# Eight attention batches inside a mixing kernel: scores kept negated and scaled in the keys, e taken a head at a time from PSUM, every sum on VectorE, and a new order

## The chip, the cores and the metric

The kernel runs on one core of one Trainium2 chip. The metric is the device time of one execution in microseconds (us); lower is better. Each time below comes from runs on such a chip, and one further execution was taken with the hardware profiler.

## What is computed

Eight heads of attention over keys and values that are pooled by eight, for eight batches of 576 tokens, and then a mixing block on the 512 channels of the result:

```python
# q, k, v: (8, 8, 576, 64)
k_p = k.reshape(B, H, 72, 8, D).mean(axis=3)
v_p = v.reshape(B, H, 72, 8, D).mean(axis=3)
scores = (1 / sqrt(64)) * q @ k_p.T
scores = scores - scores.max(-1)
attn = exp(scores)
attn = attn / (attn.sum(-1) + 1e-9)
x = (attn @ v_p).transpose(...).reshape(B, S, H * D)
theta = x @ w_theta
zr, zi = x * cos(theta), x * sin(theta)
y = einsum('ts,bsd->btd', w_tok_r, zr) + einsum('ts,bsd->btd', w_tok_i, zi)
u = x + y
out = u + maximum(u @ w_ch, 0)
```

The weights of the mixing block come as 64-bit numbers and are turned into 32-bit ones on the chip, each kept as a high and a low part.

## The kernel before

Each batch is worked in named streams of steps, and a table of words, SCHEDULE, gives the order in which the steps of all streams are issued: `S3.2` is the next step of the softmax of batch 3, tile 2, and a letter behind it (v, g, a) says whether VectorE (DVE), GpSimd (POOL) or ScalarE (ACT) does the step's work where there is a choice. The order on every engine, and much of the choice of engines, is therefore written out in the table; each engine works through its own instructions in that order and waits where an operand or a buffer is not there yet.

The streams: `k`, `v` load keys and values, `K`, `V` pool and place them (`keys` at L581 writes the tile `kpT`), `Q` brings the queries into `qT`, `S` is the softmax (`soften`, L701), `E` turns the weights e (`eraw`, `eh`, `er`) through DMAs, `X` multiplies with the values (`attend`, L904) and copies PSUM to `xT`, `T` forms theta, its sine and cosine and `z` (`rotate`, L958), `Z` splits z into `zh` and `zl`, `M` multiplies with the token weights (`mix`, L1045, matmuls `py`), `F` with w_ch (`final`, L1081, matmuls `pf`) and stores the result by way of a transpose on DVE into `R`. The streams `h`, `w`, `W`, `c` turn the weights at the start.

A softmax tile is 128 tokens (the last of five has 64) by 8 heads by 72 pooled keys. Its scores lie in two PSUM banks, of which there are two such pairs. For batches 2 to 7 a tile goes: largest score per row and head on DVE (`mx`, L762), scores less `mx` on DVE into `e_eps` (L779), one exp over all 576 columns on ACT (L783), sums on DVE (L785), their reciprocals (`ri`, L787), and the division (`en`, L792 on ACT a head at a time, or L796 on DVE or POOL; L803 for the last 8 keys). For batches 0 and 1 ACT takes exp a head at a time from PSUM, with the negated and scaled `mx` as bias, and gives the sums by its accumulator (L767 to L775). `e_eps` is one buffer, held from the first write of e to the last read of the division, and its 73rd column holds 1e-9, so that a sum over 73 columns has the small constant in it.

Four single PSUM banks serve all other matmuls. `xT` has two buffers: the copy of `pv` of batch b + 2 into `xT` (L932 on ACT, L934 on DVE) waits until the last transpose into `R` of batch b has read it (L1128).

Of the kernel before, what the change touches and what calls it, by code (L numbers as in the profile page):

```python
# [35 lines left out]
S0.1 w1.0a S0.1v S0.3 S0.4 w1.0a w0.1g h2 w1.1a w1.0a W0 h2v V0v V0 h2 w1.1a S0.4 Q1.1 S0.2 S0.2a w1.0 X0.0.0 X0.0.1
w1.1 K1.1g h3v S0.2 S0.2v w2.0v v1.0 S0.4 w2.0v X0.0.2 w1.0 h3 Q1.0 S0.3v w1.1 X0.0.1a S0.3g X0.0.2a X0.0.0a X0.0.3 K1
W0a w1.0v X0.0.3a h3v w1.1v K1a w2.1 S0.4 W1 T0.0g h3 w4.0 S0.4g w2.0a k1.2 W0 W1a S0.4g S0.3 S0.3v Q1.1 W1 S0.3 Q1.1a
Q1.0 T0.1a T0.0g T0.1v W0 S0.3a W0v S0.4 V1.0g w3.0a T0.0 Q1.0a S0.4v Q1.2 w2.1a W1 w2.0 w3.0a w2.1a w2.1v v1.1 S0.4
w2.1 w2.1 T0.0 w3.1a w2.1v T0.1 w3.0v S0.4a w2.0 w3.1v w3.1a X0.2.2 X0.2.3 T0.0 T0.0 T0.1 w2.0g T0.0 X0.2.2a X0.2.1  # L40
w3.1 K1.2g T0.1 Q1.3 V1.1g W1a T0.0a w3.1 w3.0 T0.0 X0.2.3a W0 X0.2.0 T0.0 T0.1 T0.1 X0.2.1v w3.0 T0.1a T0.0 X0.2.0a
T0.2a W1 T0.3a Q1.2 T0.1 W2 Q1.3 w3.1v Q1.2v w4.0v T0.3v V1a c0 T0.2v w4.0a w4.0a T0.1 w4.0 w3.0v Q1.3a T0.2 w4.0 W2a
Q1.4 X0.2.3g T0.2 T0.1 T0.3 T0.2 W2 c0a c0a T0.2 c0 T0.4g T0.4g T0.2 T0.3 T0.2a w4.0g W3 T0.2 T0.4 W3a T0.3 c0 T0.2
T0.3 c0 T0.3 T0.2 T0.3a K1 W2 W3 T0.4 T0.4 K1a T0.4 Q1.4 c1 T0.4 c0g W2v T0.3 c0g c0g W2 W4 V1g T0.4 T0.3 c1a T0.4
T0.3 c1a S1.0 Z0.1a Z0.0g W4v S1.0 k2.2 W4 c1 M0.1.0 Z0.1v c1 K2.2v W4a M0.1.0 M0.0.0 c1 W4 S1.0 W4a S1.0 M0.1.0
# [1216 lines left out]
```

## Time and profile before

| | |
|---|---|
| time, median of 3 runs | 567.87 us (567.5 to 568.3) |
| the profiled execution's own time | 568.15 us |
| its span | 566.3 us |
| busy PE / DVE / ACT / POOL | 546.2 / 455.6 / 330.6 / 373.2 us |
| DMA, mean over the span | 102 GB/s |

PE is TensorE's matmuls, PEld its weight loads, SP the engine that issues most DMAs. The profiled execution took 0.28 us more than the median. A row of the profile names the source line (L1058), the engine, the operation, the tile written and those read, sizes, a count and times; in brackets stands how long the engine was idle before the instruction, and what released it.

### The profile page before, as it was taken

What the parts mean: (1) busy time and instruction counts of PE and PEld (TensorE: products, weight loads), DVE (VectorE), ACT (ScalarE), POOL (GpSimd) and SP (SyncE); (2) the same over time, 40 slices, a digit from 0 to 9 for tenths busy, and PEclk for the clock granted to TensorE, in tenths of its full rate; (3) what the DMA queues carried; (4) which work ended last, traced back from release to release, by engine and by line L of the source; (5) the groups of instructions that cost most, each with busy time, mean ns of one, the idle gap of its engine ahead of it and who ended that gap; (6) DMA issues with size and microseconds to landing.
All of it is one profiled execution on the core that took longest, in us unless ns stands there. A gap on an engine that the chain in (4) does not pass through costs nothing.

```text
span 566.3 us, 11646 instructions
## 1 busy us (share of the span) xinstructions
PE 546.2 (96%) x4084; PEld 515.1 (91%) x4084; DVE 455.6 (80%) x867; ACT 330.6 (58%) x774; POOL 373.2 (66%) x526
## 2 busy tenths in 40 slices
PE   5999989999999999999989999999999999999996
PEld 5867779989999998999989999999999999999996
DVE  6999999899888798888868897987879888366164
ACT  3889988887766885566424767446354644334010
POOL 3766665587887987799867596649357766652430
PEclk9999999999999999999989999999999999999999
DMA  9988121556486775358645374543626251200017
GB/s 264 264 288 192 48 72 71 127 114 120 80 153 97 154 115 112 71 122 147 117 91 105 61 127 93 107 85 67 94 43 108 49 82 26 48 1 14 10 22 125
DMA packets 231801, 57.84 MB, mean 102 GB/s; under 512 B 218688, under 2 KB 220352, under 8 KB 231744
## 3 DMA queue, kind: packets, MB, share of 16 engines
q1 hardware_dynamic: 226768, 56.47, 49.4%
q10 hardware_dynamic: 4976, 0.64, 0.7%
q8 instruction: 32, 0.52, 0.4%
q14 instruction: 25, 0.20, 0.1%
HBM read 37.81 MB, written 9.44 MB: 83 GB/s over the span
## 4 chain that ended last, share of the span: by engine, by line
PE 66%; DVE 10%; DMA 8%; SPq 6%; POOL 4%; issue 3%; ACT 1%; DVEq 0%; POOLq 0%; ACTq 0%
PE py L1058 32%; PE pt L970 12%; PE pf L1091 11%; PE pv L923 4%; PE s L728 3%; PE px L984 2%; DMA kpst<-in_k_dram 2%; SPq L878 2%; DMA WTh_st<-in_moe_w_theta_dram 2%; DMA wraw<-in_moe_w_tok_r_dram 2%; DMA vpst<-in_v_dram 1%; SPq L608 1%; DMA out_dram<-R 1%; SPq L629 1%; DVE en L803 1%
## 5 line engine op out<-in xcount | busy, mean ns | idle before, releaser
L1058 PE MATMUL py<-WTh,zh 128*128 128x288 f32 x576 | 81.8, 288 | 1.7 <-ACT zh L206 1.7
L1058 PE MATMUL py<-WTh,zl 128*128 128x288 f32 x576 | 83.0, 292 | 0.0
L1058 PE MATMUL py<-WTl,zh 128*128 128x288 f32 x576 | 81.2, 287 | 0.0
L191 POOL TENSOR_TENSOR zl<-z,zh 128x256 fp32r<-128x256 f32 (+2 forms) x80 | 63.5, 825 | 22.3 <-ACT zh L206 13.2
L1058 PEld LDWEIGHTS py<-WTh,zh 128*128 128x128 f32 x576 | 74.8, 189 | 2.4 <-ACT zh L206 1.9
L1058 PEld LDWEIGHTS py<-WTh,zl 128*128 128x128 f32 x576 | 76.2, 193 | 0.1
L1058 PEld LDWEIGHTS py<-WTl,zh 128*128 128x128 f32 x576 | 74.8, 189 | 0.2
L976 ACT ACTIVATE g<-pt,c_magic 128x512 f32<-128x512 f32 x35 | 24.0, 687 | 52.9 <-PE pt L970 40.9
L1068 DVE TENSOR_TENSOR xT<-py,xT 128x288 f32<-128x288 f32 x64 | 27.9, 444 | 28.4 <-PE py L1058 28.0
L191 POOL TENSOR_TENSOR ul<-xT,uh 128x288 fp32r<-128x288 f32 x42 | 34.0, 823 | 22.1 <-DVE uh L208 12.2
L1091 PE MATMUL pf<-uh,chh 128*128 128x288 f32 x256 | 43.7, 293 | 0.0
L1091 PE MATMUL pf<-uh,chl 128*128 128x288 f32 x256 | 41.9, 286 | 0.0
L1091 PE MATMUL pf<-ul,chh 128*128 128x288 f32 x256 | 41.8, 286 | 0.0
L970 PE MATMUL pt<-th,xh 128*128 128x512 f32 x148 | 39.4, 389 | 0.6 <-POOL Vl L191 0.6
L1098 DVE SCALAR_TENSOR_TENSOR xT<-pf,xT 128x288 f32<-128x288 f32 x64 | 28.1, 446 | 14.5 <-PE pf L1091 14.1
L728 PE MATMUL s<-kpT,qT 128*128 128x144 f32 x256 | 36.9, 288 | 1.9 <-ACT kpT L206 0.8
L970 PE MATMUL pt<-th,xl 128*128 128x512 f32 x148 | 38.2, 381 | 0.2 <-DVE xl L964 0.2
L792 ACT ACTIVATE en<-e_eps,ri 128x64 f32<-128x64 f32 (+1 forms) x120 | 30.3, 335 | 13.3 <-DVE ri L787 9.5
L970 PE MATMUL pt<-tl,xh 128*128 128x512 f32 x148 | 38.0, 379 | 0.0
L762 DVE TENSOR_REDUCE mx<-s 128x8 f32<-128x576 f32 (+2 forms) x42 | 29.9, 715 | 9.6 <-PE s L728 9.4
L1091 PEld LDWEIGHTS pf<-uh,chh 128*128 128x128 f32 x256 | 36.1, 190 | 0.6
L728 PEld LDWEIGHTS s<-kpT,qT 128*128 128x128 f32 x256 | 33.6, 190 | 3.1 <-issue 1.1
(268 smaller groups left out, 1438.8 us busy)
## 6 DMA issues: line engine op xcount, KB each, us to landing
out_dram<-R SPq DMA_DIRECT2D x112, 72.0 KB, 2.1
kpst<-in_k_dram SPq DMA_DIRECT2D x15, 512.0 KB, 4.1
vpst<-in_v_dram SPq DMA_DIRECT2D x28, 256.0 KB, 3.8
qsst<-in_q_dram SPq DMA_DIRECT2D x96, 72.0 KB, 2.4
eraw<-G SPq DMA_DIRECT2D x96, 60.0 KB, 2.2
eraw<-G SPq DMA_DIRECT2D x96, 40.0 KB, 2.0
WTh_st<-in_moe_w_theta_dram SPq DMA_DIRECT2D x4, 512.0 KB, 7.1
wcraw<-in_moe_w_ch_dram SPq DMA_DIRECT2D x4, 512.0 KB, 3.4
```

Source lines behind the costliest of these rows:

```text
L191: nc.gpsimd.tensor_tensor(out[:, r], a[:, r], b[:, r], op)
L728: nc.tensor.matmul(scs[c // 2][:n, 2 * SP * (c % 2) : 2 * SP * (c % 2 + 1)], qT[:, c, t0 : t0 + n], kpT[:, c, :], start=True, stop=True,)
L762: nc.vector.tensor_reduce(mxv, scv, AX.X, ALU.max)
L792: nc.scalar.activation(en[:n, GM * h : GM * h + GM], e[:n, h, 0:GM], AF.Copy, scale=ri[:n, h : h + 1])
L878: nc.sync.dma_start(blocks(Ex, jj, i), blocks(Gx, i, jj))
L923: nc.tensor.matmul(as_written(pv[:, :gn]) if pair else pv[:, :gn], l, by_turns(r) if pair else r, start=i == 0, stop=i == len(terms) - 1,)
L970: nc.tensor.matmul(as_written(pt), l[:, c, :], by_turns(r[:, c, :]), start=i == 0, stop=i == 11)
L976: nc.scalar.activation(halves(g), in_order(pt), AF.Identity, bias=c_magic)
L1058: nc.tensor.matmul(as_written(py[:, :n]), l[:, kk, :], by_turns(r[:, kk, t]), start=i == 0, stop=i == 3 * NK - 1,)
L1068: nc.vector.tensor_tensor(halves(u), in_order(py[:, :n]), halves(u), ALU.add)
L1091: nc.tensor.matmul(as_written(pv[:, :n]), l[:, kk, o], by_turns(uhl[r][:, kk, t]), start=i == 0, stop=i == 11,)
L1098: nc.vector.scalar_tensor_tensor(halves(oT), in_order(pv[:, :n]), 0.0, halves(oT), ALU.max, ALU.add)
```

## The change

Keys are multiplied by -1/64 when they are copied from PSUM into `kpT` (new helper `scaled`; on DVE or ACT). The scores then come out negated and scaled, so the row's minimum takes the maximum's place, exp is taken of minus the score plus that minimum, and neither the subtraction nor the negation of `mx` is needed. For every batch e is taken a head at a time from PSUM on ACT (eight instructions a tile), without the accumulator; all sums are DVE reductions. With `EACH` always true, the branch with the subtraction is never taken. The table is another one throughout: the order of all steps and the engines of many.

```diff
-EARLY, EXACT, V_ON_PE, K_ON_PE, Q_ON_PE, SUMS_ON_ACT = 2, 1, 1, 1, 2, 2
+EARLY, EXACT, V_ON_PE, K_ON_PE, Q_ON_PE, SUMS_ON_ACT = 2, 1, 1, 1, 2, 0
+EACH = lambda b, m: True
...
+    def scaled(e, out, src, by):
+        if e == "a":
+            nc.scalar.activation(out, src, AF.Copy, scale=by)
+        else:
+            nc.vector.tensor_scalar(out, src, by, None, ALU.mult)
...
     def keys(b):
+        by = -1.0 / (POOL * math.sqrt(D))
...
-        copy(e, kpT[0:64, :, 0:SP], heads[:, 0::2])
-        copy(e, kpT[64:128, 0:3, SP:], heads[:, 1::2])
+        scaled(e, kpT[0:64, :, 0:SP], heads[:, 0::2], by)
+        scaled(e, kpT[64:128, 0:3, SP:], heads[:, 1::2], by)
...
         for scv, mxv, _, _ in views:
-            nc.vector.tensor_reduce(mxv, scv, AX.X, ALU.max)
+            nc.vector.tensor_reduce(mxv, scv, AX.X, ALU.min)
...
-        if b < SUMS_ON_ACT:
-            nc.scalar.mul(mx[:n], mx[:n], -scale)
+        if each:
             yield
+            sums = dict(accum_out=sm[:n]) if b < SUMS_ON_ACT else {}
             for x in range(8):
                 j, y = at(x)
                 nc.scalar.activation(
                     e[:n, x], scs[j][:n, SP * y : SP * y + SP], AF.Exp,
-                    bias=mx[:n, x : x + 1], scale=scale, accum_out=sm[:n, x : x + 1],
+                    bias=mx[:n, x : x + 1], scale=-1.0, **{w: s[:, x : x + 1] for w, s in sums.items()},
                 )
-            nc.scalar.activation(sm[:n], sm[:n], AF.Identity, bias=c_eps[:n])
...
+        if b >= SUMS_ON_ACT:
+            if split:
+                nc.vector.tensor_reduce(sm[:n], e[:n], AX.X, ALU.add)
+                nc.vector.tensor_scalar(sm[:n], sm[:n], 1e-9, None, ALU.add)
+            else:
+                nc.vector.tensor_reduce(sm[:n], e_eps[:n], AX.X, ALU.add)
```

Three places where the order moves follow. The first is DVE where batch 4's first copies into `xT` wait for batch 2's last transposes into `R`: `en_4` is the last softmax tile of batch 4, `mx_2` and `sm_2` belong to batch 5. Before:

```order
L785 TENSOR_REDUCE sm_4_3771<-e_eps 64x8
L787 RECIPROCAL ri_4_3917<-sm_4_3771 64x8
L796 TENSOR_TENSOR en_4_3919<-e_eps,ri_4_3917 64x512
L1128 STREAM_TRANSPOSE R_3_3887<-xT_2220 128x288
L1128 STREAM_TRANSPOSE R_2_3922<-xT_2220 128x288
L803 TENSOR_TENSOR en_4_3919<-e_eps,ri_4_3917 64x64
L1128 STREAM_TRANSPOSE R_2_3922<-xT_2220 128x288
L812 STREAM_TRANSPOSE G<-en_4_3919 64x4x128
L815 STREAM_TRANSPOSE G<-en_4_3919 64x64
L762 TENSOR_REDUCE mx_2_3941<-s_2_3882 128x8
L779 TENSOR_TENSOR e_eps<-s_2_3882,mx_2_3941 128x8x72
L785 TENSOR_REDUCE sm_2_3943<-e_eps 128x8
```

and the change, in the same place:

```order
L801 TENSOR_REDUCE sm_4_3715<-e_eps 64x8
L803 RECIPROCAL ri_4_3974<-sm_4_3715 64x8
L1114 SCALAR_TENSOR_TENSOR xT_2290<-pf_3_0_3950,xT_2290 128x288
L1144 STREAM_TRANSPOSE R_3_3980<-xT_2290 128x288 x2
L771 TENSOR_REDUCE mx_2_3984<-s_2_3967 128x8
L950 TENSOR_SCALAR xT_3924<-pv_0_2_3925 128x256
L828 STREAM_TRANSPOSE G<-en_4_4011 64x4x128
L831 STREAM_TRANSPOSE G<-en_4_4011 64x64
L771 TENSOR_REDUCE mx_3_4072<-s_3_3900 128x8
L801 TENSOR_REDUCE sm_2_3986<-e_eps 128x8
```

The division of `en_4` has left DVE (POOL does both parts of it now), the subtraction L779 is gone, the next tile's minimum comes ahead of this tile's sum, and one of the four copies into `xT` has come to DVE.

The second is ACT at the same place, with `xT<-pv` the copies of batch 4. Before:

```order
L783 ACTIVATE e_eps<-e_eps 64x8x72
L206 CAST zh_2_3926<-z_3531 128x1152
L932 ACTIVATE xT_3891<-pv_0_0_3929 128x256
L932 ACTIVATE xT_3891<-pv_0_1_3892 128x256
L783 ACTIVATE e_eps<-e_eps 128x8x72
L932 ACTIVATE xT_3891<-pv_0_3_3974 128x256
L206 CAST uh_4002<-xT_2946 128x288
```

and the change:

```order
L948 ACTIVATE xT_3924<-pv_0_1_3930 128x256
L948 ACTIVATE xT_3924<-pv_0_0_3945 128x256
L209 CAST zh_0_4039<-z_3577 128x1152
L781 ACTIVATE e_eps<-s_2_3967,mx_2_3984 128x72 x8
L209 CAST uh_4139<-xT_3013 128x288
L781 ACTIVATE e_eps<-s_3_3900,mx_3_4072 128x72 x8
L948 ACTIVATE xT_3924<-pv_0_3_4024 128x256
```

Where one exp of 576 columns stood, eight of 72 stand, and the second block of eight stands ahead of the copy of `pv_0_3`.

The third is SP at the start of the program, where the loads of the first keys (`kpst`, `early`, `kprst`), of the first weights (`WTh_st`, `wraw`) and of the first queries (`qsst`) are issued. Before:

```order
L519 DMA kpst_0_117<-in_k_dram 128x2x512
L519 DMA early<-in_k_dram 128x2x512
L387 DMA WTh_st<-in_moe_w_theta_dram 128x1024
L438 DMA wraw_0_144<-in_moe_w_tok_r_dram 128x1152
L531 DMA kprst_149<-in_k_dram 64x512
L629 DMA qsst_0_163<-in_q_dram 128x8x64
```

and the change:

```order
L447 DMA wraw_0_117<-in_moe_w_tok_r_dram 128x1152
L528 DMA kpst_0_119<-in_k_dram 128x2x512
L396 DMA WTh_st<-in_moe_w_theta_dram 128x1024
L540 DMA kprst_128<-in_k_dram 64x512
L528 DMA early<-in_k_dram 128x2x512
L396 DMA WTh_st<-in_moe_w_theta_dram 128x1024
```

The token weights have gone from fourth place to first, and the second load of keys from second to fifth.

## Rows read from the trace of the kernel before

**Rows 1.** The page, parts 1 and 2: busy time by engine, busy tenths in 40 slices.

```profile
PE 546.2 (96%) x4084; PEld 515.1 (91%) x4084; DVE 455.6 (80%) x867; ACT 330.6 (58%) x774; POOL 373.2 (66%) x526
...
DVE  6999999899888798888868897987879888366164
...
PEclk9999999999999999999989999999999999999999
```

**Rows 2.** Busy time (instructions) of PE, PEld, DVE, ACT, POOL in seven stretches.

```profile
0.00:30.00 30.00, 22.71 (x182) 19.95 (x183) 23.70 (x50) 18.29 (x79) 16.14 (x26) 1.00 1.01 262
30.00:80.00 50.00, 47.16 (x284) 36.25 (x283) 48.78 (x84) 46.08 (x100) 33.90 (x43) 1.00 0.55 156
80.00:150.00 70.00, 68.55 (x531) 65.16 (x530) 63.73 (x129) 56.44 (x174) 47.22 (x74) 1.00 0.48 102
150.00:280.00 130.00, 128.26 (x969) 122.45 (x967) 109.62 (x203) 86.89 (x193) 109.77 (x154) 1.00 0.66 122
280.00:300.00 20.00, 18.08 (x144) 17.64 (x143) 15.42 (x25) 5.22 (x9) 13.21 (x20) 0.91 0.39 76
300.00:560.00 260.00, 259.53 (x1972) 252.22 (x1971) 192.10 (x375) 117.70 (x222) 152.97 (x212) 1.00 0.38 65
560.00:566.00 6.00, 1.90 (x15) 1.43 (x13) 2.22 (x8) 0.00 (x0) 0.00 (x0) 0.93 0.59 122
```

**Rows 3.** Timeline 278 to 296: start, us, instruction, idle before it and releaser.

```profile
281.96 3.09 POOL L191 TENSOR_TENSOR zl<-z,zh 128x384 fp32r<-128x384 f32 x4
281.97 4.53 DVE L803 TENSOR_TENSOR en<-e_eps,ri 64x64 f32<-64x64 f32 x1
...
285.02 2.20 POOL L191 TENSOR_TENSOR vpst<-vpst 128x256 f32<-128x256 f32 x3
...
286.98 0.66 ACT L932 ACTIVATE xT<-pv 128x256 f32<-128x256 f32 x2 [9.00 <-DVE R L1128]
...
287.42 0.38 PE L923 MATMUL pv<-eh,Vh 128*128 128x256 f32 x1 [1.92 <-ACT xT L932]
...
288.42 4.05 PE L1058 MATMUL py<-WTh,zl 128*128 128x288 f32 x18
```

**Rows 4.** Chain that ended last, 370 to 490: start, us, what.

```profile
375.72 2.21 PE py L1058 x18
```

**Rows 5.** Groups by line, softmax on DVE: count, busy us, mean ns, idle before.

```profile
L762 DVE TENSOR_REDUCE mx<-s 128x8 f32<-128x576 f32 x30 | 22.4, 746 | 9.6 <-PE s L728 9.4
...
L779 DVE TENSOR_TENSOR e_eps<-s,mx 128x576 f32<-128x576 f32 x24 | 18.2, 758 | 1.7 <-ACT en L792 0.3
L785 DVE TENSOR_REDUCE sm<-e_eps 128x8 f32<-128x584 f32 x24 | 18.0, 750 | 3.7 <-ACT e_eps L783 3.7
```

**Rows 6.** The same groups on ACT.

```profile
L792 ACT ACTIVATE en<-e_eps,ri 128x64 f32<-128x64 f32 (+1 forms) x120 | 30.3, 335 | 13.3 <-DVE ri L787 9.5 <-DVE G L815 3.6
...
L783 ACT ACTIVATE e_eps<-e_eps 128x576 f32<-128x576 f32 (+1 forms) x30 | 20.5, 685 | 20.8 <-DVE e_eps L779 20.6
L771 ACT ACTIVATE e_eps<-s,mx 128x72 f32<-128x72 f32 (+1 forms) x64 | 19.4, 331 | 0.0
...
L767 ACT ACTIVATE mx<-mx 128x8 f32<-128x8 f32 (+1 forms) x10 | 2.0, 200 | 4.4 <-DVE mx L762 4.4
```

**Rows 7.** Timeline of the start, PE and ACT.

```profile
5.01 3.75 PE L575 MATMUL kpp<-kpst,ident 128*128 128x128 f32 x16 [5.01 <-DMA kpst<-in_k_dram]
...
78.83 1.37 PE L1058 MATMUL py<-WTh,zh 128*128 128x288 f32 x9 [1.73 <-ACT zh L206]
...
9.50 0.78 ACT L356 ACTIVATE wsrc_a<-wraw 128x576 f32<-128x576 f32 x1 [4.35 <-DMA wraw<-in_moe_w_tok_r_dram]
```

**Rows 8.** Per line: count, ns of one as min/median/max, of three DVE lines.

```profile
L779 DVE TENSOR_TENSOR e_eps<-s,mx x30: 749/758/760, 126.5 to 476.1; 128x576 f32<-128x576 f32 x24, 64x576 f32<-64x576 f32 x6
L803 DVE TENSOR_TENSOR en<-e_eps,ri x19: 175/482/4531, 87.4 to 471.3; 128x64 f32<-128x64 f32 x15, 64x64 f32<-64x64 f32 x4
L1075 DVE TENSOR_TENSOR ul<-xT,uh x22: 431/454/1290, 127.2 to 550.0; 128x288 fp32r<-128x288 f32 x22
```

More of the change, by code (lines that the diff above doesn't have):

```diff
@@ L36 @@
[L36 to L45, printed above, removed]
@@ new lines @@
+S1.1 S1.1 Q2.0 M0.2.1 S1.1a S1.4 Z0.3g S1.1 X1.0.0 S1.2a V2.2g S1.2v M0.2.1 X1.0.2 k2.0 M0.2.0 M0.2.1 K2.0g Q2.0
+X1.0.1 X1.0.2v X1.0.0v X1.0.1v S1.3 S1.3 S1.2 S1.4 X1.0.3 X1.0.3a S1.2a S1.2 M0.3.1 M0.0.1a T1.0g S1.2 S1.3a k2.1
+M0.3.1 S1.3v T1.0g Q2.0 S1.4 M0.3.1 S1.3 S1.3v M0.3.1 S1.3 T1.0 M0.2.1a S1.4 K2.1v M0.3.0 S1.3 S1.2a T1.0 M0.3.1a
+T1.1g M0.0.0a Q2.1 T1.0 M0.3.0 S1.3a S1.2 S1.4g v2.0 S1.4g K2 S1.3 T1.1g M0.3.0 T1.0 K2v S1.4 T1.0 T1.0a M0.3.1g
+M0.3.0 M0.1.1v M0.3.0g M0.0.0g T1.0 V2.0g S1.4v Q2.1 S1.4 S1.4 S1.4a v2.1 T1.0 T1.0 M0.1.0g S1.4 T1.1 X1.2.1 k3.2 K2
@@ new lines @@
+T2.2a V3 E3.2 F1.0.1 T2.1 F1.0.0 F1.1.0 T2.1a S3.0g T2.1 F1.1.1 F1.0.0 E3.2 F1.3.1 T2.3g T2.1 T2.2g T2.2 F1.1.1 S3.1
+E3.2 T2.1 Q4.0 T2.3g F1.1.1 S3.1 F1.0.1 V3g F1.3.1 F1.2.0 T2.2 T2.2 V3g E3.2g S3.1 F1.3.0 E3.2a F1.3.0 T2.2 F1.1.1
+Q4.1 K4 T2.2 T2.2a F1.2.0 S3.0 E3.2g F1.2.1 T2.2 T2.2 E3.2g F1.2.1 T2.2 F1.3.0 S3.1g T2.3 K4a F1.2.1 Q4.1 F1.2.0
+F1.3.1 T2.3 v4.0 S3.1v X3.2.2 X3.2.2a X3.2.3 T2.3 X3.2.0 X3.2.0v X3.2.3a X2.2.3g X3.2.1 S3.1 X3.2.1a X3.2.3a E3.0 T2.3
+T2.3 T2.4v T2.3a Q4.1 T2.3 T2.3 K4.2g T2.4g K4 T2.4 T2.3 Z2.0v Z2.0v E3.0 K4a v4.2 T2.4 S4.1 T2.4 S4.0 S4.1 T2.4
@@ new lines @@
+v5.0 T3.0 S4.2a K5 M2.3.0 K5a M2.1.0v T3.1g Q5.0 M2.3.0a S4.3 T3.2v E4.0 S4.2g E4.0 T3.0 T3.0 M2.2.1 M2.2.1 M2.2.0
+T3.0a K5 E4.0 V4v T3.0 M2.2.1g M2.2.0 S4.3 T3.0 V5.0g T3.1 K5v M2.2.0v M2.1.0v M2.0.0v T3.0 T3.2g T3.3v T3.1 T3.1
+M2.3.0g T3.1 T3.1 T3.1a T3.1 M2.3.1 V4 M2.3.1 T3.2 M2.2.0g M2.3.1 E4.0 S4.4 F2.1.0 T3.1 T3.1 M2.0.1g M2.3.1 T3.2
+F2.0.0 F2.1.0 S4.2 T3.2 T3.3g V4g T3.4a M2.2.1g T3.2 M2.3.1a F2.0.0 M2.3.1v T3.2 Q5.1 F1.3.1 E4.0v S4.3 F2.1.0 T3.2a
+T3.2 E4.0a Q5.1 V4g F2.1.1 F2.0.1 E4.0g E4.0g T3.2 F2.0.1 F2.0.1 v5.2 F2.1.1 T3.3 T3.2 F2.1.1 v5.1 F2.3.1 T3.3 T3.3
@@ new lines @@
+T4.1 F3.0.1 F3.3.0 F3.3.1 F3.3.0 F3.0.0 S5.1 V5v T4.2g Q6.1 T4.1 F3.0.1 V6.0g F3.2.0 T4.2 T4.1 F3.3.1 T4.1v T4.1 K6
+T4.1 F3.1.1 E5.2a S5.1 T4.1 S5.0 F3.1.0 F3.1.1 F3.2.1 F3.2.0 T4.2 K6a T4.2 T4.2 E5.2g E5.2g T4.3g T4.2 E5.2g F3.2.1
+F3.2.1 T4.3 V5g T4.2a T4.2 v6.1 T4.2 T4.2 K6 F3.2.0 S5.1g X5.2.3 F3.3.1 F3.3.0 K6v T4.3 X5.2.3a X5.2.2 X5.2.1 T4.3
+Q6.1 S5.1v X5.2.0 X5.2.2a X5.2.0v T4.3 T4.3 S6.1 S5.1 X5.2.1a T4.3a X5.2.3g T4.4v T4.3 S6.0 T4.4g T4.3 T4.4 T4.3 T4.4
+E5.0 Z4.0v T4.4 T4.4 Z4.0g Z4.0g T4.4 Z4.0g T4.4a T4.4 T4.4 V6.1g M4.0.0 E5.0 T4.4 E5.0 Z4.0v M4.0.0 M4.0.1 M4.0.0
@@ new lines @@
+S6.2 T5.1 S6.3 M4.3.0g T5.3v E6.0 S6.4 S6.2g M4.0.0g T5.1 Q7.0 T5.2 M4.3.1 T5.1a M4.3.1 S6.2v M4.2.0g E6.0 E6.0g
+M4.0.0g T5.1 T5.1 S6.3 M4.1.1g M4.0.1v M4.2.1 E6.0g V6g T5.1 T5.2 T5.4a Q7.1 T5.2 M4.3.0v T5.2 M4.2.1 F4.3.0 k7.1
+F3.3.1 Q7.1 T5.2 M4.3.1 K7.1g S6.3 T5.2v M4.3.1g v7.0 M4.2.1 T5.2 k7.2 T5.3 V6 F4.1.0 T5.2 M4.2.1g M4.2.1g T5.2 S6.2
+F4.3.0 F4.1.0 M4.3.1v T5.3 T5.3 F4.0.0 F4.0.0 E6.0g F4.1.0 T5.3 T5.3 K7 T5.3a F4.3.1 K7a F4.1.1 T5.3 F4.3.0 F4.0.1
+T5.3 T5.3 V6g F4.3.1 S6.3g F4.1.1 F4.1.1 Z5.0g F4.2.1 S6.3g K7.2g M5.0.0 Q7.1 S6.4 K7 Z5.0g F4.3.1 F4.1.1 K7v S6.3
@@ new lines @@
+S7.4 F4.2.1 F4.2.0 V6v F4.2.0 S7.2 S6.4 F4.0.1 S6.4v E6.0g F4.2.0 F4.3.1 M5.0.0 Z5.1a M5.0.0 S6.4g M5.0.1 F4.0.0
+M5.0.1 F4.0.1 X6.0.0 M5.0.1 M5.0.0 S7.2 Z5.1g X6.0.1 F4.2.1 S7.2 M5.0.1 Z5.3g X6.0.0v X6.0.2 X6.0.3 S6.4 M5.1.0
+X6.0.1a S7.3 M5.1.0 v7.2 X6.0.3v M5.3.0 F4.0.1 E6.2 X6.0.2v E6.2 S7.3 S7.2 M5.1.0 Z5.3g E6.2 M5.3.1 S7.2a S7.2v T6.1g
+M5.1.1 M5.1.0 M5.0.1v S7.3 T6.0v T6.1v M5.1.1 S7.0 S7.3 M5.1.1 Z5.2a M5.0.0v S7.4 V7.2v Z5.2v M5.3.0 T6.0g M5.1.1 T6.0
+T6.0 V7.0g E6.2 S7.2 S7.3v M5.3.1 E6.2v T6.0 M5.3.1 M5.3.1 S7.3g E6.2g M5.2.0 M5.3.0 M5.2.1 M5.2.0 M5.2.0 M5.2.1 S7.4
@@ new lines @@
+F6.2.1 F6.2.0 T7.1 Z7.0v F6.0.0 Z7.2g M7.2.0 M7.0.0 F6.1.0 M7.2.0 Z7.2v M7.2.0 M7.2.0 M7.0.0 F6.1.1 M7.2.1 Z7.0v
+F6.2.0 M7.0.0 F6.3.0 M7.2.1 M7.2.1 Z7.1g M7.0.1 M7.2.1 M7.0.1 F6.3.1 F6.1.0 M7.2.1v F6.3.0 Z7.1v F6.3.0 M7.1.0 F6.3.1
+M7.0.1 M7.2.0a M7.1.0 M7.1.1 M7.0.0 M7.1.1 M7.1.0 Z7.3v M7.3.0 M7.0.0v Z7.3v M7.1.0 M7.1.0v F6.0.0 M7.3.1 M7.2.0g
+M7.3.0 M7.3.0 M7.3.1 M7.1.1 M7.0.0v M7.3.0 M7.3.0g M7.1.1 F6.0.1 M7.0.1 M7.3.1 M7.0.1a M7.1.0g M7.3.0v M7.3.1 F6.0.1
+M7.3.1v F7.1.0 F7.0.0 M7.3.1v M7.1.1a F7.0.0 M7.1.1g F6.1.1 M7.0.1v F7.1.0 F6.2.1 M7.2.1v F6.2.0 F6.2.1 F7.1.0 F7.1.0
@@ L590, in keys @@
         heads = pk[0:64].rearrange("p c x -> p (c x)")[:, 0 : 7 * SP].rearrange("p (h g) -> p h g", g=SP)
-        copy(e, kpT[0:64, :, 0:SP], heads[:, 0::2])
-        copy(e, kpT[64:128, 0:3, SP:], heads[:, 1::2])
-        copy(e, kpT[64:128, 3, SP : 2 * SP - GM], pk[0:64, 3, P - GR :])
+        scaled(e, kpT[0:64, :, 0:SP], heads[:, 0::2], by)
+        scaled(e, kpT[64:128, 0:3, SP:], heads[:, 1::2], by)
+        scaled(e, kpT[64:128, 3, SP : 2 * SP - GM], pk[0:64, 3, P - GR :], by)
         yield
@@ L597, in keys @@
         yield
-        copy(pick(), kpT[64:128, 3, 2 * SP - GM :], pr[0:64, 0:64])
+        scaled(pick(), kpT[64:128, 3, 2 * SP - GM :], pr[0:64, 0:64], by)
         yield
@@ L706, in soften @@
         nt, mi = len(tiles), m - tiles[0]
-        scale = 1.0 / (POOL * math.sqrt(D))
         split = b == 0 and m % 2
@@ L761, in soften @@
         for scv, mxv, _, _ in views:
-            nc.vector.tensor_reduce(mxv, scv, AX.X, ALU.max)
-        if b == 0:
+            nc.vector.tensor_reduce(mxv, scv, AX.X, ALU.min)
+        each = b < SUMS_ON_ACT or EACH(b, m)
+        if not each and b == 0:
             yield
         sm = work([P, 8], F32, "sm", f"sm{b}_{m}", bufs=2)
-        if b < SUMS_ON_ACT:
-            nc.scalar.mul(mx[:n], mx[:n], -scale)
+        if each:
             yield
+            sums = dict(accum_out=sm[:n]) if b < SUMS_ON_ACT else {}
             for x in range(8):
@@ L772, in soften @@
                     e[:n, x], scs[j][:n, SP * y : SP * y + SP], AF.Exp,
-                    bias=mx[:n, x : x + 1], scale=scale, accum_out=sm[:n, x : x + 1],
+                    bias=mx[:n, x : x + 1], scale=-1.0, **{w: s[:, x : x + 1] for w, s in sums.items()},
                 )
-            nc.scalar.activation(sm[:n], sm[:n], AF.Identity, bias=c_eps[:n])
+            if sums:
+                nc.scalar.activation(sm[:n], sm[:n], AF.Identity, bias=c_eps[:n])
             yield
@@ L782, in soften @@
             yield
-            nc.scalar.activation(e[:n], e[:n], AF.Exp, scale=scale)
+            nc.scalar.activation(e[:n], e[:n], AF.Exp, scale=-1.0)
             yield
-            nc.vector.tensor_reduce(sm[:n], e_eps[:n], AX.X, ALU.add)
+        if b >= SUMS_ON_ACT:
[4 more added lines that the diff above has]
+                nc.vector.tensor_reduce(sm[:n], e_eps[:n], AX.X, ALU.add)
         ri = work([P, 8], F32, "ri", f"ri{b}_{m}", bufs=2)
```

167 lines of the change are left out of this document (71 added, 96 removed).

## The prediction

> **What bounds the kernel now.** I began with the page's parts 1 and 2 [rows 1]. PE is busy 546.2 us of a span of 566.3, DVE 455.6, POOL 373.2, ACT 330.6. The change does not touch the list of matmuls (the same products, in another order), so all that it can win or lose lies in the some 20 us in which PE is idle, and in stretches where PE's clock is low. A busy share alone tells nothing of those 20 us, so I next cut the span into seven windows [rows 2]. PE idles 7.3 us in 0 to 30, 2.8 in 30 to 80, 1.45 in 80 to 150, 1.7 in 150 to 280, 1.9 in 280 to 300, 0.5 in 300 to 560 and 4.1 in the last 6. Three things are to be seen. From 300 on, PE is busy 259.53 of 260 us at full clock: nothing can be won there, only lost. From 30 to 80, DVE is busy 48.78 of 50 us and ACT 46.08: there these two set the pace, until the first `py` starts at 78.83 us, after a wait of 1.73 us on ACT's `zh` [rows 7]. And only one window has a low mean clock, 280 to 300 with 0.91.
>
> The timeline of that window [rows 3] shows why. DVE's `en` of 64x64 (L803) starts at 281.97 and takes 4.53 us; POOL runs `zl` and then `vpst` from 281.96 on. Behind that division on DVE stands a transpose into `R`, the last reader of the `xT` buffer; ACT waits 9.00 us for it before the copy of `pv` at 286.98, and PE waits 1.92 us for ACT. [...]
>
> **The change part by part.** The profiled execution took 568.15 us, 0.28 more than the median of the runs; the sum is made against 568.15.
>
> *The stall at 282 to 292.* In the new order `en_4` is on POOL, whole, and the two transposes that stood around it on DVE are no longer split by it. Then PE's wait (1.92) and the slow `py` (4.05 − 2.21 = 1.84) go: **−3.8 us**. Late next there is ACT: its copy of `pv_0_3` now stands behind a second block of eight exps, some 2 us (below). Only one of four copies waits for that block, and PE has `py` and `pf` to work on meanwhile, so I take nothing off. Bounds: 0 if another late hand-over takes its place, −3.8 if none does.
>
> *The scaled keys.* The copies to `kpT` are the same in number, with a multiplication in place of a plain copy. No row shows the price of that, but these are PSUM reads of one pass like the plain copies, which have no second operand tile either: 0, and at worst one L767 (200 ns, ACT's multiplication of a small tile [rows 6]) for each of a batch's four, under 1 us a batch and beside PE.
>
> *The softmax of batches 2 to 7.* DVE loses 30 subtractions of 0.758 us (24 of the large shape make 18.2 us, the six small ones cost as much by their minimum of 749 [rows 5, 8]): 30 × 0.758 = −22.7. It gains the sums of batches 0 and 1, ten at 0.750 [rows 5], +7.5. ACT pays eight exps of 72 columns for one of 576. The plain one takes 0.685 [rows 6]. The nearest rows to the new ones are L771, 19.4 us busy for 64, 0.303 each with the accumulator, and L792, 30.3 for 120, 0.253 each, 64 columns without it. The new ones have no accumulator, so I take 0.253: 8 × 0.253 = 2.0 us a tile, +1.3 for each of 30 tiles, +40 us on ACT; the other end is 8 × 0.303 = 2.4. In batches 0 and 1 ACT loses the accumulator, its ten small multiplications L767 (2.0 us [rows 6]) and ten additions. The chain of a tile goes from minimum, subtraction, exp, sum (0.746 + 0.758 + 0.685 + 0.750 = 2.94) to minimum, eight exps, sum (0.746 + 2.0 + 0.750 = 3.5), 0.56 us longer. From 150 us on the cover is PE's own queue: between the scores of one tile and those of the next PE has `py`, `pf` and transposes to do, of which 18 `py` alone are 2.21 us [rows 4], and there are two pairs of score banks. From 300 to 560 DVE has 68 us idle and ACT 142 [rows 2]. So I cost this at **0** there. Were the cover gone, 30 × 0.56 = 17 us would be the price. `e_eps` stays one buffer: where DVE's subtraction waited for the last tile's division, ACT's exps now do, and behind them on ACT stand `xT` copies and `zh`, for which PE waits. That is a rival below.
>
> *The start.* Ahead of the first `py` DVE has five sums more (+3.7 at 0.750 [rows 5]), and against them copies into `qT`, `eraw` and `Ve`, three scalings of `th` and two of `wsrc_a` that now go to ACT or come later. Summed over all instructions that differ, each at the mean of its like in the trace, DVE's work ahead of the first `py` falls by 0.6 us and ACT's rises by 0.1. POOL's falls. DVE is the fullest there (48.78 of 50 [rows 2]), so: **−0.6 us**. The DMA queue gives both bounds. `wraw` first, ahead of `kpst`, ends ACT's wait of 4.35 us for it at 9.50 [rows 7], of which ACT, nearly as full as DVE, might make 2 us of gain. But PE's first work waits 5.01 us for `kpst` [rows 7], and `wraw`'s 128 × 1152 words of four bytes, 576 KB, now go ahead of it: at the 262 GB/s of the first 30 us [rows 2] that is up to 2.2 us later. Between −2 and +2.2 the count of DVE's work is the nearest.
>
> *80 to 280.* PE idles 3.2 us here in all [rows 2], which is the most that a better order could give back: −3. Ahead of a same count of matmuls DVE has some 6 us less to do (part of the subtractions, filled only partly with work from POOL) and ACT some 3 us more; ACT has 13.6 us free of 70 in 80 to 150 [rows 2]. I take **0**, with −3 and +4 (one stall as in rows 3) as bounds.
>
> *300 to the end.* PE is full; the last 4.1 us (the store of the last result) stay. **0**.
>
> The sum: 568.15 − 3.8 − 0.6 = 563.8, against the median 563.5. I forecast **563.6 us**; with the bounds of start and middle its own range is 560.5 to 566.
>
> [...] The rows show L803, which reads `e_eps` and `ri` from SBUF, once at 4531 ns where its median is 482 [rows 8], while POOL reads SBUF; L1075, also of two SBUF tiles, once at 1290 with a median of 454; and L779, whose one operand is in PSUM, never above 760 in 30 [rows 8]. [...]
>
> **The rivals.** *The same time, by new stalls* (0.16). An order drawn anew can put a late hand-over where there was none: one more like that of rows 3 gives back 3.8 us, so 567 to 569. For it: 30 of the tiles' chains are 0.56 us longer, and PE has no slack to make up for what it loses. Against it: six batches in sequence follow one pattern, and the old order had a single such place.
>
> *Slower, by blocked divisions and additions on DVE* (0.16). By the new order DVE has 179 two-operand instructions with both operands in SBUF, before 140: 39 more, and 30 fewer with one in PSUM. In the trace of before, those of the first kind are the ones with outliers (4531 and 1290 [rows 8]), those of the second have none. The mechanism: a blocked instruction on DVE ahead of the last `R` transpose of a batch, with the `xT` copy, and so PE, waiting behind. It decides once the block outlasts what PE has queued: in rows 3 a delay of 4.5 us cost 3.8. If two of the five such hand-overs (batches 3 to 7, with that of batch 4 gone) are hit, 563.8 + 2 × 3.8 = 571.4 us. Against it: 39 more in 140 is a quarter, and one such hit was seen in all of before, so two are few times as likely as none.
>
> *Slower, by ACT* (0.14). In 80 to 150 ACT is busy 56.44 of 70 us [rows 2]; the new exps add 1.3 us a tile in front of copies of `pv` and of `zh`, and they wait in order for `e_eps`. If four such copies come 2 us late (one block of exps each) with PE waiting, 563.8 + 8 = 571.8. It decides where a block stands directly ahead of a copy that PE needs within 2 us, as with `pv_0_3`. For it: PE's first `py` waits on ACT already [rows 7]. Against it: from 150 on ACT idles a third and more [rows 2]. [...]
>
> **How the numbers follow.** My forecast has 0.54. About 0.2% (1.1 us) is what a measurement here can tell from no change. Faster by more is below 566.7: the forecast's own range, 0.54. Within 0.2%: the first rival, 0.16. Slower: the two rivals by DVE's blocks and by ACT (0.16 and 0.14), 0.30. The range reaches down to 559.5 (all bounds of gain together: 568.15 − 3.8 − 2 − 3 = 559.4) and up to 571.5, which takes in the blocked DVE and leaves out ACT's worse half.
>
> **What would show it.** Right: no DVE instruction of over 2 us around the copies of batch 4, PE's clock at 1.00 all through 150 to 560, `e_eps<-s,mx` near 0.25 us each, the first `py` at about 78, PE idle under 1 us from 300 to 560. Wrong: a window of 20 us after 150 with a mean clock below 0.95 or over 1 us of PE idle, released by ACT's `xT` copy (then look whether a DVE instruction of two SBUF operands or a block of exps stands ahead of it); or a first `py` after 80 us, with `kpst` as the releaser of PE's first work.

## The result, and the profile after

The change is slower: 573.29 us median of 4 runs (572.08 to 575.91) against 567.8 before, a ratio of 1.0098 with a 95% interval of 1.007 to 1.0126. The profiled execution took 573.11 us with a span of 571.3, 5.0 more than before.

The page's part 1 and the clock row of part 2, for the change:

```profile
PE 548.5 (96%) x4084; PEld 518.4 (91%) x4084; DVE 460.1 (81%) x883; ACT 348.0 (61%) x877; POOL 342.2 (60%) x488
...
PEclk9999989999999999999999999899989999999999
```

Its stretches, in the columns of [rows 2]:

```profile
30.00:80.00 50.00, 47.04 (x292) 36.53 (x291) 47.68 (x86) 47.86 (x108) 29.76 (x37) 0.99 0.53 149
80.00:150.00 70.00, 69.30 (x529) 66.33 (x528) 62.69 (x128) 61.92 (x176) 53.81 (x82) 0.98 0.49 102
150.00:280.00 130.00, 127.52 (x968) 122.57 (x967) 112.08 (x212) 91.18 (x240) 94.64 (x137) 1.00 0.65 119
280.00:300.00 20.00, 20.00 (x166) 19.46 (x165) 14.83 (x30) 8.17 (x26) 11.98 (x16) 1.00 0.48 91
300.00:560.00 260.00, 255.18 (x1911) 247.41 (x1910) 196.04 (x371) 119.94 (x283) 139.72 (x199) 0.99 0.36 63
```

Up to 280 us nothing is lost: PE's 196.82 us between 80 and 280, for 1497 matmuls, stand against 196.81, for 1500, in [rows 2]. The old stall is gone, 280 to 300 is full at clock 1.00. The loss is after 300, where PE had been full: it is now busy 255.18 of 260 us. It lies in two places, which the clock row shows as its 8s in the slices that begin at 357 and 414 us (the 8 in the slice from 71 us lies around the first `py`, ahead of the loss). The same view, cut around them:

```profile
352.00:366.00 14.00, 12.18 (x87) 11.99 (x86) 11.64 (x24) 11.10 (x34) 5.37 (x8) 0.88 0.62 124
404.00:422.00 18.00, 15.57 (x122) 14.90 (x121) 14.75 (x23) 2.42 (x10) 13.19 (x17) 0.91 0.33 55
```

The timeline of the second place (columns as in [rows 3]):

```profile
410.56 0.29 POOL L194 TENSOR_TENSOR en<-e_eps,ri 64x64 f32<-64x64 f32 x1 [1.95 <-DVE ri L803]
410.67 3.79 DVE L812 TENSOR_TENSOR en<-e_eps,ri 64x512 f32<-64x512 f32 x1
410.82 3.09 POOL L194 TENSOR_TENSOR zl<-z,zh 128x384 fp32r<-128x384 f32 x4
...
413.90 1.56 POOL L211 CAST zh<-z 128x1152 fp32r<-128x1152 f32 x1
414.38 1.18 DVE L1144 STREAM_TRANSPOSE R<-xT 128x288 f32<-128x288 f32 x3
415.50 0.41 DVE L1084 TENSOR_TENSOR xT<-py,xT 128x288 f32<-128x288 f32 x1
...
415.96 0.38 PE L939 MATMUL pv<-eh,Vh 128*128 128x256 f32 x1 [1.75 <-DVE xT L1084]
...
417.35 0.58 PE L939 MATMUL pv<-eh,Vh 128*128 128x256 f32 x1 [0.68 <-DVE xT L1084]
```

The division of batch 6, tile 4 (the row of 64x512) takes 3.79 us on DVE; the six others of its line in the change take 0.69 to 1.29, and the same division undisturbed takes 0.73 (below, label pool_behind). It ends at 414.46, 0.55 us after POOL's four `zl`, a little less than its free length. Behind it on DVE stand three transposes and the addition of `py` into `xT`, which frees the PSUM bank that the next `pv` needs. PE waits 1.75 and 0.68 us, and from 416 to 422 us the granted clock reads 0.72, where it read 1.00 from 404 to 416.

The first place, one batch earlier:

```profile
358.75 0.73 DVE L510 TENSOR_TENSOR vprst<-vprst 64x256 f32<-64x256 f32 x2 [0.50 <-DMA vprst<-in_v_dram]
...
359.30 3.11 POOL L194 TENSOR_TENSOR zl<-z,zh 128x384 fp32r<-128x384 f32 x4 [0.49 <-ACT zh L209]
...
359.51 0.90 DVE L515 TENSOR_TENSOR vpr<-vprst 64x64 f32<-64x64 f32 x1
360.34 0.76 DVE L819 TENSOR_TENSOR en<-e_eps,ri 128x64 f32<-128x64 f32 x1
361.03 0.44 DVE L1084 TENSOR_TENSOR xT<-py,xT 128x288 f32<-128x288 f32 x1
...
361.52 0.38 PE L939 MATMUL pv<-eh,Vh 128*128 128x256 f32 x1 [1.82 <-DVE xT L1084]
```

Two small DVE instructions beside POOL's `zl` take 0.90 and 0.76 us here, and PE waits 1.82 us for the addition behind them; the clock reads 0.63 from 361.4 to 366, after 1.00 from 352 to 361.4.

Against the same matmuls in the run with both places mended (below, label both), the change needs 44.43 us in place of 40.67 from the start of the 177th `pv` to that of the 1081st `py`, and 40.80 in place of 36.53 from there to the 209th `pv`: 3.8 and 4.3 us. The start of the change:

```profile
6.66 3.76 PE L584 MATMUL kpp<-kpst,ident 128*128 128x128 f32 x16 [6.66 <-DMA kpst<-in_k_dram]
...
78.14 1.47 PE L1074 MATMUL py<-WTh,zh 128*128 128x288 f32 x9 [1.97 <-POOL zh L211]
```

PE's first matmul is 1.65 us later than in [rows 7], the first `py` 0.7 earlier. From the start of the last matmul to the end of the span it is 4.7 us where it was 3.5. In all: −0.7 (start) −3.8 (282 to 292) +3.8 +4.3 (the two places) +1.2 (end) = +4.8, of the 5.0 seen between the two profiled executions.

### The profile page after: what moved, and what is told of

The parts are those of the page before. It is cut to its first block, busy times and chain, and to the rows that moved or that the text cites. A ratio compares the mean times of both kernels' runs of the same rounds, so it can differ in the third digit from the quotient of the medians.

```text
span 571.3 us, 11725 instructions
## 1 busy us (share of the span) xinstructions
PE 548.5 (96%) x4084; PEld 518.4 (91%) x4084; DVE 460.1 (81%) x883; ACT 348.0 (61%) x877; POOL 342.2 (60%) x488
## 4 chain that ended last, share of the span: by engine, by line
PE 68%; DVE 9%; SPq 6%; ACT 6%; POOL 4%; DMA 3%; issue 3%; DVEq 0%; ACTq 0%; POOLq 0%
PE py L1074 30%; PE pf L1107 12%; PE pt L986 10%; SPq L894 5%; PE s L737 5%; PE pv L939 4%; PE px L1000 2%; PE kpp L584 1%; DMA kpst<-in_k_dram 1%; DMA vprst<-in_v_dram 1%; PE s L729 1%; ACT wsrc_a L365 1%; PE vpp L584 1%; SPq L1159 1%; DVE sm L801 1%
## 5 line engine op out<-in xcount | busy, mean ns | idle before, releaser
L1074 PE MATMUL py<-WTh,zh 128*128 128x288 f32 x576 | 83.6, 294 | 2.0 <-POOL zh L211 2.0
L781 ACT ACTIVATE e_eps<-s,mx 128x72 f32<-128x72 f32 (+1 forms) x304 | 67.9, 333 | 28.3 <-DVE mx L771 14.1
L1074 PE MATMUL py<-WTl,zh 128*128 128x288 f32 x576 | 83.6, 291 | 0.0
L1074 PE MATMUL py<-WTh,zl 128*128 128x288 f32 x576 | 81.1, 289 | 0.8 <-DVE zl L1058 0.8
L1074 PEld LDWEIGHTS py<-WTh,zh 128*128 128x128 f32 x576 | 77.1, 195 | 2.4 <-POOL zh L211 2.1
L194 POOL TENSOR_TENSOR zl<-z,zh 128x256 fp32r<-128x256 f32 (+2 forms) x60 | 47.2, 818 | 11.3 <-ACT zh L209 7.3
L211 POOL CAST zh<-z 128x1152 fp32r<-128x1152 f32 (+2 forms) x14 | 15.3, 1090 | 48.3 <-PE py L1074 22.6
L194 POOL TENSOR_TENSOR en<-e_eps,ri 128x256 f32<-128x256 f32 (+3 forms) x53 | 28.5, 555 | 22.2 <-DVE ri L803 9.3
L994 DVE SCALAR_TENSOR_TENSOR g<-g,pt 128x512 f32<-128x512 f32 x35 | 23.7, 678 | 16.4 <-ACT g L992 16.2
L194 POOL TENSOR_TENSOR xl<-xT,xh 128x256 fp32r<-128x256 f32 x40 | 31.0, 796 | 9.8 <-DVE xh L211 7.6
```

The lines of the kernel that those rows point to most:

```text
L194: nc.gpsimd.tensor_tensor(out[:, r], a[:, r], b[:, r], op)
L211: ENG[e].tensor_copy(out, src)
L781: nc.scalar.activation(e[:n, x], scs[j][:n, SP * y : SP * y + SP], AF.Exp, bias=mx[:n, x : x + 1], scale=-1.0, **{w: s[:, x : x + 1] for w ...
L994: nc.vector.scalar_tensor_tensor(halves(g), halves(g), MAGIC, in_order(pt), ALU.subtract, ALU.subtract)
L1074: nc.tensor.matmul(as_written(py[:, :n]), l[:, kk, :], by_turns(r[:, kk, t]), start=i == 0, stop=i == 3 * NK - 1,)
```

## The experiments

**The division alone, to ACT** (theory A: DVE instructions held up by POOL at two places; B: the softmax itself; C: the order itself, blocks or not).

```diff
-S6.4v
+S6.4a
```

> The change with one letter of the table altered: the division of batch 6, tile 4, for 64 keys a head (3.79 us on DVE at 410.67, where its like takes 0.69 to 0.82) goes to ACT, which is idle for 12.3 us there. Theory A: PE's waits of 1.75 and 0.68 us at 416 and the low clock after them go, 573.3 less some 4.5: 568 to 570 us. Theory B: 573 us or more, since ACT gets more to do. Theory C: DVE is only shorter by the unblocked 0.7 to 0.8 us: 572 to 573.3.

568.31 us (565.19 to 572.16), ratio 1.0007 (0.9977 to 1.0036); between 404 and 422 us PE is busy all 18.00. As A: one instruction moved gives 5.0 us back.

**POOL made to come behind the division.** That run could have worked by relieving DVE. So here DVE keeps everything, and only POOL is made to wait:

```diff
+        if (b, m) == (6, 4):
+            nc.gpsimd.tensor_copy(late[:n], en[:n, 0:1])
```

> The change with one small instruction added: POOL copies one column of the division's result (batch 6, tile 4) ahead of the zl that ran beside it, so POOL waits until DVE has divided. DVE's work and its order stay as they are. Theory A (the division was held up because POOL ran zl): it takes 0.7 to 0.9 us in place of 3.79, POOL's zl comes some 1 us later, which nobody waits for, PE's waits at 416 go: 568 to 570 us. Theory C (late by order, or held up by something other than POOL): the division keeps some 3.8 us or the wait stays, 573 us or more.

568.67 us, ratio 1.0018 (0.999 to 1.0047). Its timeline:

```profile
409.15 0.73 DVE L812 TENSOR_TENSOR en<-e_eps,ri 64x512 f32<-64x512 f32 x1
...
409.81 1.18 DVE L1146 STREAM_TRANSPOSE R<-xT 128x288 f32<-128x288 f32 x3
409.95 0.18 POOL L826 COPY late<-en 64x1 f32<-64x1 f32 x1 [0.61 <-DVE en L812]
410.09 3.09 POOL L194 TENSOR_TENSOR zl<-z,zh 128x384 fp32r<-128x384 f32 x4
...
410.93 0.41 DVE L1086 TENSOR_TENSOR xT<-py,xT 128x288 f32<-128x288 f32 x1
```

The same division takes 0.73 us and PE doesn't wait. More work on POOL, none less on DVE, and 4.6 us faster: the block is shown, and C falls for this place.

**The division in another form**, on DVE, in its place:

```diff
+        elif (b, m) == (6, 4):
+            for h in range(8):
+                nc.vector.tensor_scalar(en[:n, GM*h : GM*h+GM], e[:n, h, 0:GM], ri[:n, h:h+1], None, ALU.mult)
```

> The change with the one division of 410.67 us left on DVE at its place, but written as eight instructions with one tile operand each and a scalar of the row (64 columns a piece, some 0.1 to 0.2 us each) instead of one with two tile operands. Theory A (it is the second operand from SBUF that is blocked while POOL runs zl): the eight take 0.8 to 1.6 us in all, the wait of 1.75 us at 416 is gone or under 0.3 us, 568 to 571 us. If any work of DVE is held up there while POOL runs: the eight take 3 us or more and the time stays at 573.

577.25 us, ratio 1.0155 (1.0131 to 1.0178): worse. The line's own view (ns as min, median, max) and its timeline:

```profile
L813 DVE TENSOR_SCALAR en<-e_eps,ri x8: 238/756/4360, 411.4 to 418.9; 64x64 f32<-64x64 f32 x8
```

```profile
411.38 7.80 DVE L813 TENSOR_SCALAR en<-e_eps,ri 64x64 f32<-64x64 f32 x8
...
420.68 0.58 PE L944 MATMUL pv<-eh,Vh 128*128 128x256 f32 x1 [6.34 <-DVE xT L1089]
```

The theory of the second operand was wrong: these pieces have one tile operand. A free piece takes 0.238 us; the first took 4.36, through four `zl` and a cast of POOL, and the median of the eight is 0.756, about one `zl` (3.04 us for four, from 415.77). Yet not all of DVE is held up: in the change's profile transposes, `xT<-py` and a minimum, of one SBUF tile or with an operand in PSUM, run in 0.19 to 0.73 us between 415.5 and 418.4, beside four `zl` (3.07 us from 415.54). The run also gives the price in three steps: with no block 568.3 us, with 3.79 us 573.3, with 7.80 us 577.3.

**The first place: the last values of batch 6 pooled on POOL**, alone and with the division on ACT.

```diff
-V6.2v
+V6.2g
```

> The change with one letter of the table altered: the pooling of the last values of batch 6 (two additions of 0.36 us and one of 0.90 on DVE at 358.75 to 360.4, the last beside POOL's zl) goes to POOL, which stands idle 0.49 us just before. DVE's next additions into xT, for which PE waits 1.82 us at 361.5, then come some 1.6 us or more earlier. Theory A: that wait and the low clock after it go, 573.3 less some 3.5: 569 to 571 us, if POOL's zl is not late for py instead. Theory B: 573 us. Theory C: the wait shrinks by the unblocked 1.0 us alone and the time by 1 to 2: 571.5 to 572.5.

> The change with both letters altered: the division of batch 6, tile 4, on ACT and the last values of batch 6 pooled on POOL. If the two stalls are independent, as theory A has it: 573.3 less 5.0 (measured by the one) less 3.6 (by the PE work between 358 and 403 us in the other's trace) makes 564.7; 563.5 to 566.5 us. If the stall at 360 only moves the wait to the one at 412 (theory C), 567.5 to 569 us, no better than the one alone.

Alone: 573.06 us, ratio 1.0083 (1.0048 to 1.0117), no gain in the median, although the wait is gone in its profile (352 to 366: PE busy all 14.00). In that profile two other stretches take back what the first place gives: the first `py` came 2.1 us later than in the change, with nothing altered ahead of it, and from the 1081st `py` to the 209th `pv`, around the second place, it needs 42.12 us in place of 40.80, with the clock at 0.81 from 404 to 422. Both: 567.47 us, ratio 1.0005 (0.9983 to 1.0027), 0.8 below the division alone; its profiled execution took 564.62, its slowest run 569.98. The expectation of 564.7 was met by that one execution and not by the median. So in the median the change with both places mended is no faster than the kernel before: some 3 us that the sum above would give (567.8 − 0.7 − 3.8 + 1.2 = 564.5) are missing, and no run shows where. The start, which comes out in two ways (last section), may be part of it.

**POOL behind DVE at both places.** Does the block make the first stall, or the late `vprst` and the order?

```diff
+        if (b, m) == (6, 0):
+            nc.gpsimd.tensor_copy(late0[:n], en[:n, 512:513])
```

> pool_behind, and the same treatment at the other place: POOL copies one column of the last part of the division of batch 6, tile 0 (0.76 us on DVE at 360.34, where its like takes 0.18 to 0.22) ahead of its next zl, so that zl comes behind DVE's vpr and en; DVE's work and order are as in the change. Theory A (DVE held up by POOL makes most of this stall too): vpr takes 0.2 to 0.3 and en 0.2 us, PE's wait of 1.82 us at 361.5 falls by 1.2 to some 0.6 or less, and the time to 566 to 568 us. Theory C (at this place it is DVE's order and the late load of vprst): the wait stays above 1.2 us, 568 to 569 us as pool_behind.

567.19 us, ratio 0.9973 (0.9951 to 0.9995). Its timeline:

```profile
362.48 0.22 DVE L515 TENSOR_TENSOR vpr<-vprst 64x64 f32<-64x64 f32 x1
...
362.62 0.21 DVE L819 TENSOR_TENSOR en<-e_eps,ri 128x64 f32<-128x64 f32 x1
...
363.25 0.38 PE L943 MATMUL pv<-eh,Vh 128*128 128x256 f32 x1 [0.19 <-DVE xT L1088]
...
363.47 3.10 POOL L194 TENSOR_TENSOR zl<-z,zh 128x384 fp32r<-128x384 f32 x4
```

0.90 and 0.76 us have become 0.22 and 0.21, and the wait of 1.82 is 0.19. A holds here too. In time this place is worth 1.5 us by the medians (568.67 to 567.19), hardly clear of the scatter, since the intervals of the two ratios just meet, and 0.8 us by the run with both letters. That is below the 3.8 of the change's profile: in the profiles of en4_6_on_act and pool_behind, where it is untouched, PE waits 1.5 us there, not 1.82, and the clock is 1.00, not 0.88. So the fall of the clock doesn't always follow.

**The old stall, undone in the kernel before.**

```diff
-S4.4v ... S4.4v
+S4.4g ... S4.4g
```

> The kernel before with two letters altered: the division of batch 4, tile 4, goes from DVE to POOL as in the change, both parts of it. Theory A: the stall at 282 to 292 goes (1.92 us of wait, 1.84 of low clock), 567.9 less 3.8: 563.5 to 565 us. If the stall were a matter of the order and not of the blocked division: 567 to 568.5 us.

563.86 us (562.15 to 566.67), ratio 0.9931 (0.9904 to 0.9958): 3.7 us, as forecast. Its timeline and stretch:

```profile
283.91 1.44 POOL L191 TENSOR_TENSOR en<-e_eps,ri 64x256 f32<-64x256 f32 x3
...
285.51 0.66 ACT L932 ACTIVATE xT<-pv 128x256 f32<-128x256 f32 x2 [5.24 <-PE pv L923]
```

```profile
280.00:300.00 20.00, 20.00 (x176) 19.78 (x175) 14.57 (x29) 5.60 (x10) 18.60 (x27) 1.00 0.43 87
```

This is the fastest version, ahead of both kernels: the one gain of the change, without the rest.

**The parts apart: the new softmax in the old order, and the old softmax in the new order.**

```diff
-SCHEDULE = """ (the change's)
+SCHEDULE = """ (that of before, without the step of L767)
```

> The order and the engines of the kernel before, with the whole change of the softmax and keys in it (keys times -1/64, minimum, eight exps of 72 columns a tile from PSUM, all sums on DVE). Theory A (blocked DVE instructions at two places of the new order make the loss; the softmax is beside the path): 566 to 569 us, because the stall at 282 to 292 has its division still on DVE. Theory B (the softmax itself loses: eight exps, 1.8 us of ACT for 0.685, come late for PE): 571 us or more. Theory C (the new order hands over late by its own order, blocks or not): as A.

> The order of before with the new softmax, but the sums of batches 0 and 1 by ACT's accumulator as before; the keys are scaled and batches 2 to 7 have their eight exps. Theory D (the 16 us that the new softmax lost in the old order are ten sums on DVE in the full start, some 14 us by 165 us, and a score bank that is held until ACT's exps, 4 to 7 us at 364): the start is as before, first py at 78 to 80 us, and the stall at 364 stays, 571 to 575 us. Theory B (eight exps a tile lose in all batches): 578 us or more. Theory A as first stated (softmax beside the path): 566 to 569.

583.7 us, ratio 1.0286 (1.0214 to 1.0359): here theory A as first stated is wrong, the softmax is not beside the path. In its profile, of an execution of 589.72, the first `py` comes at 87.3 us, 8.5 later than before. With the accumulators kept for batches 0 and 1 it is 577.05, ratio 1.0154 (1.0123 to 1.0186), and the first `py` is at 77.6: so ten sums on DVE, in place of ACT's accumulator, cost that order 6.7 us by the medians. What is left shows in the waits of PE (us in total, times, longest) and in the timeline, for old_order_acc01:

```profile
PE s L736 <- ACT e_eps L780: 6.0, 3, 4.3
...
PE s L728 <- ACT e_eps L780: 1.5, 1, 1.5
```

```profile
350.06 0.75 DVE L770 TENSOR_REDUCE mx<-s 128x8 f32<-128x576 f32 x1
...
354.15 0.72 ACT L1014 ACTIVATE g<-g,c_cos 128x512 f32<-128x512 f32 x1
...
354.89 1.28 ACT L780 ACT_TABLE_LOAD   x1
...
356.18 1.80 ACT L780 ACTIVATE e_eps<-s,mx 128x72 f32<-128x72 f32 x8
...
358.03 2.29 PE L736 MATMUL s<-kpT,qT 128*128 128x144 f32 x8 [4.29 <-ACT e_eps L780]
```

The minimum is ready at 350.81, but ACT, in order behind sine and cosine and then behind a table load of 1.28 us (ACT_TABLE_LOAD), takes e only at 356.18, and PE's next scores wait 4.29 us for the bank. These waits for e are 7.5 us in all, of the 9.5 that this run loses against the kernel before. In the kernel before none of PE's larger waits is for e: there DVE's subtraction was the last reader of the scores. Theory D (sums and bank) gave the mechanisms; its 571 to 575 was 2 us low.

> The order and the engines of the change, with the softmax of before in it (maximum, subtraction on DVE, one exp of 576 columns, accumulator for batches 0 and 1). Theory A: 571 to 576 us; DVE has 22.7 us more to do in the same order, and the two places of blocked instructions stay. Theory B: 569 us or less. Theory C: 571 us or more, as A.

> As new_order_old_softmax, with the subtraction of a tile issued in its exp's step and no longer in its maximum's, so that it comes behind the last tile's sums (there it was issued ahead of them and overwrote e, so the values of that run are not the reference's). If the new order suits only the new softmax: 580 us or more, some of it ahead of the first py, where ACT has the accumulators again. If only the two places of theory A cost time in the new order: 571 to 576 us.

The first of the two issues a tile's subtraction ahead of the last tile's sums and so overwrites their e: it has the work of this mixture but not its result, and only the second computes the same as the two kernels. 593.27 us, ratio 1.0454 (1.0386 to 1.0522), and 598.28, ratio 1.0517 (1.0418 to 1.0616). In the second profile the first `py` comes at 85.3 us. Each order suits its own softmax: each full mixture loses over 15 us.

**The loads at the start**, on top of both:

```diff
-w0.0 k0.0 h1
+k0.0 w0.0 h1
```

> The change with both letters altered (567.5 us) and the first load of keys put ahead of the first load of token weights. If DVE and ACT set the pace up to the first py, as the prediction has it: PE's first matmul comes at 5.0 in place of 6.1 to 6.7 us, the first py moves by under 0.5, 567 to 568 us. If the loads set it: the first py some 1 to 1.6 us earlier, 566 to 566.5 us. If ACT's wait for the token weights comes back (4.35 us in the kernel before) and is on the path: slower, 569 us or more.

566.67 us, ratio 0.997 (0.9944 to 0.9996), 0.8 below both. In its profile PE starts at 4.5 us, but the first `py` is at 79.3 where it was 77.8. The early start of PE did not reach the first `py` in that run; the 0.8 is less than the scatter of these runs and is left open.

## Why the prediction was wrong

The forecast was 563.6 us, faster; the time is 573.29, beyond the range's end of 571.5.

- *The stall at 282 to 292*, −3.8: right in cause and size, by the stretch 280 to 300 and by 3.7 us when only that division is moved. Its 1.84 is the 18 `py` of [rows 3] less those of [rows 4]; from 287.4 to 293 us, where the slow ones run, the granted clock reads 0.70 before, and in the change 1.00 over the same stretch.
- *The start*, −0.6: the change's profile gives −0.7, but the closeness is luck. In seven profiles with this order of loads, and nothing altered ahead of it, the first `py` comes at 77.8 to 80.9 us, against 78.83 in [rows 7] and 79.45 in before_en4_on_pool. PE's later first matmul was hidden, as chosen between the bounds. But sums are not cheap there, as the old order shows (6.7 us for the ten); what pays for them in the new order no run shows.
- *80 to 280*, 0: right, 196.82 against 196.81 us.
- *The softmax, 0, on the ground that its chain is only 0.56 us longer*: right for the new order alone. The exps cost less than assumed, 0.225 us each (the change's groups on ACT and DVE by form, columns as in [rows 5, 6]), and the sums what was assumed:

```profile
L781 ACT ACTIVATE e_eps<-s,mx 128x72 f32<-128x72 f32 x240 | 53.9, 337 | 22.3 <-DVE mx L771 14.1 <-DVE en L819 5.2 <-POOL en L194 2.8
...
L801 DVE TENSOR_REDUCE sm<-e_eps 128x8 f32<-128x584 f32 x30 | 22.4, 748 | 4.9 <-ACT e_eps L781 4.8
```

  The working looked at the length of the chain and left out who frees the score banks: it was DVE's subtraction, and is now ACT's last exp, in order behind other work.
- *"300 to the end. PE is full", 0*: **this step failed.** PE full at clock 1.00 in [rows 2] said that the old order had no late hand-over there, not that a new one would have none. Two hand-overs behind blocked DVE instructions cost 3.8 and 4.3 us in the profile, and the median falls from 573.29 to 567.47 us when both are taken away. The other 3.9 us of the miss are not in this step, and of them only the 1.2 us of the end below are placed.
- The end, taken as unchanged, costs 1.2 us more.

Two slips in the working bear on the range. The bounds of start and middle give 568.15 − 3.8 + 2.2 + 4 = 570.6 at the upper end, not 566, and with the stall's own bound of 0 they give 574.4, which takes in the measured time. And batches 3 to 7 without batch 4 are four hand-overs, not five.

The second rival, blocked divisions and additions on DVE, is what happened: two hits, and 571.4 us by its working. The hand-over was another (the addition of `py` into `xT`, which frees a bank for `pv`, and not the `xT` copy). Its chance of 0.16 came from a count of all such instructions, 39 more in 140. The new table held a better one: where such a DVE instruction stands directly ahead of a hand-over, and whether POOL has a run of `zl` at that place. [Rows 8] set two SBUF operands apart from one in PSUM; the eight pieces with one tile operand, from SBUF, were held up as well, up to 4360 ns (en4_6_one_operand). What decides which instruction is held up, no run shows.

## What to carry to other kernels

In this kernel PE was full from 300 to 560 us [rows 2], so there was nothing to win there and much to lose: when an order is drawn anew, look on each in-order engine for the last instruction ahead of each hand-over, and ask what could hold it up. On DVE, a division from SBUF beside a run of POOL work took five times its length (3.79 us for 0.73); making POOL wait for it by a copy of one column gave back 4.6 us without moving any work. And when a pass is taken away, ask which buffer it released.
